# The order of a planned attention-and-gating kernel: one greedy pass against four backward-and-forward passes

## Chip, core and metric

The kernel runs on one core of a Trainium2 chip. The metric is the device time of one execution in microseconds (us). TensorE is called PE here and in the rows, VectorE DVE, ScalarE ACT, GpSimd POOL and SyncE SP. "PEld" is the weight-load side of PE.

## What is computed

The reference chains an attention that keeps only the 32 best scores of each row, a gated block that mixes along the sequence, and a gated block with a causal convolution, all in float32:

```
# q, k, v: 4 x 8 x 576 x 64
scores = scale * np.matmul(q, k.transpose(0, 1, 3, 2))
kth = np.partition(scores, -32, axis=-1)[..., -32:-31]
scores = np.where(scores >= kth, scores, -1e9)
attn = softmax(scores);  x = attn @ v          # laid out as 4 x 576 x 512
h = relu(x @ w_in);  u, v = h[..., :512], h[..., 512:]
v_n = (v - mean(v)) / sqrt(var(v) + 1e-6)
x = (u * (w_spatial @ v_n + b_spatial)) @ w_out
gate = sigmoid(causal_conv5(x, conv_w))
out = (gate * (x @ w_val)) @ w_out2
```

## The kernel before

The attention is cut into 72 units, 18 for each of the 4 batch rows; a unit is two blocks of 128 query rows against all 576 keys. For each unit PE computes the scores in two halves (L453, into the one PSUM tile `sps`), and ACT copies each half to SBUF (L456, `sb`, three buffers). DVE then finds the 32nd largest score of every row: it folds the scores to 168 candidates (L472 to L484, `tm`, `cand`), takes the 8 largest (L494, `t8a`), and three times strikes out the 8 found and takes the next 8 (L505, L507, `t8b`). ACT has meanwhile made the exponentials (L499, `e`, two buffers); DVE masks them with the threshold and sums them (L524), takes the reciprocal of the sum (L529, behind a small ACT copy L528), ACT scales (L532), PE transposes (L541 and L546), ACT copies out (L543, L548), PE multiplies by v (L562), ACT stores into `xt` (L568).

The two gated blocks ("moe" in the code) follow for each batch row as pieces: `xsplit` splits the input into a high and a low part (L623, L625), `piece_v` and `piece_u` are the two halves of the first product (matmuls of helper L603), `piece_sp` the product along the sequence (L706, gated on DVE in L711), `piece_x2`, `conv` (L755), `piece_val` (gated on DVE in L783) and `piece_out`. Their matmuls run as three products of high and low parts. The pieces of one batch row run among the attention units of the next row; those of the fourth row have no attention left beside them. In the first row's attention, the weights, which come as 64-bit numbers, are decoded on ACT, DVE and POOL (`decode`, L292 to L313, and `decode_spatial`) and written to DRAM; `w_load` (L381) loads them again from POOL's queue into one of two buffers `wblk`.

Nothing of the order on the engines is written by hand. Every step is entered with `od.add`: its engine, an estimated duration, the buffers that it reads and writes, a tag with a due time in units (`at`), and in some cases a second engine that could do it (`alt`: the clamp L297 and the low part L298 of `decode`, and for the last batch row the copies and subtractions of the pieces). `Order.plan` plays the steps once through a model of the engines: whenever an engine is free, it takes, of the steps that are ready, the one with the smallest due time plus `AHEAD[tag]`, a table of 45 offsets. `run` then issues the steps in the order in which they were taken. Each engine works its instructions off in that order, so a step that waits holds up all that stand behind it on its engine.

## Time and profile before

| | |
|---|---|
| time, median of 3 runs | 850.48 us (847.73 to 852.22) |
| time of the profiled execution | 852.4 us |
| its span, first to last instruction | 850.5 us |
| busy: PE / DVE / ACT / POOL | 722.2 / 752.4 / 607.0 / 281.0 us |
| mean granted clock of TensorE | 0.927 of full speed |
| instructions | 17268 |

The span is what the trace covers; the time of the same execution holds 1.9 us more around it. Busy times of engines overlap, so they don't add up to the span. An idle time in a row, with what ended it, stands in square brackets.

### The profile page before, as it was taken

To read this page: it belongs to the slowest core of one execution; us is meant where nothing else is said; L and a number is where in the kernel's file an instruction comes from. 1 tells how busy PE (TensorE), PEld (TensorE's weight loads), DVE (VectorE), ACT (ScalarE), POOL (GpSimd) and SP (SyncE) were. 2 spreads that over 40 slices of the span, in tenths; PEclk is the share of its full clock that TensorE was granted. 3 is DMA by queue.
4 is the path that set the end of the run, shared out by engine and by line. 5 is a ranking of instruction groups with operands and counts; after the bars stand their busy time and mean duration, and the time that the engine had idled before them with its cause. 6 is when DMAs were issued, how large, how long until landed. Compare 5 with 4: busy or idle time off the path is not lost.

```text
span 850.5 us, 17268 instructions
## 1 busy us (share of the span) xinstructions
PE 722.2 (85%) x5969; PEld 615.5 (72%) x5969; DVE 752.4 (88%) x2751; ACT 607.0 (71%) x1391; POOL 281.0 (33%) x350
## 2 busy tenths in 40 slices
PE   3153656775979999999999999979999999999987
PEld 2142445554769888987889888857888999878975
DVE  5999999999999999999999999996989999941580
ACT  5477966677887667777986777668786777774341
POOL 5685342576423211222333211213334122322120
PEclk9995766666989999999999999999999999999989
DMA  8777333224114511243224411234035005333501
GB/s 246 255 262 267 100 118 101 77 87 131 51 30 150 188 58 30 99 152 109 79 72 169 156 29 59 91 145 147 16 125 189 25 2 197 139 118 131 207 2 60
DMA packets 46954, 99.25 MB, mean 117 GB/s; under 512 B 22532, under 2 KB 29960, under 8 KB 43272
## 3 DMA queue, kind: packets, MB, share of 16 engines
q0 software_dynamic: 4032, 53.74, 17.7%
q1 hardware_dynamic: 42824, 44.31, 16.6%
q8 instruction: 49, 0.80, 0.4%
q14 instruction: 49, 0.40, 0.2%
HBM read 79.88 MB, written 18.15 MB: 115 GB/s over the span
## 4 chain that ended last, share of the span: by engine, by line
PE 47%; DVE 28%; ACT 15%; POOL 4%; DMA 3%; issue 3%; SPq 0%; POOLq 0%; ACTq 0%; DVEq 0%
PE mp L603 14%; PE xr L562 7%; PE sps L453 6%; PE mp L706 6%; PE mp L755 6%; DVE e L524 5%; DVE tw L505 4%; PE ptp L541 4%; DVE t8b L507 3%; ACT e L532 3%; ACT e L499 2%; ACT pt L543 2%; DVE gate L766 2%; DVE cand L481 2%; DVE tm L473 2%
## 5 line engine op out<-in xcount | busy, mean ns | idle before, releaser
L453 PE MATMUL sps<-k,q 64*128 64x144 f32 (+1 forms) x1280 | 126.7, 341 | 47.9 <-ACT sb L456 40.5
L453 PEld LDWEIGHTS sps<-k,q 64*128 64x128 f32 (+1 forms) x1280 | 90.9, 202 | 78.5 <-ACT sb L456 51.9
L541 PE MATMUL ptp<-ident,e 128*128 128x128 f32 x576 | 94.9, 307 | 51.1 <-ACT e L532 50.4
L524 DVE SCALAR_TENSOR_TENSOR e<-sb,t8b,e 128x576 f32<-128x576 f32 x144 | 128.1, 921 | 1.3 <-ACT e L499 1.3
L541 PEld LDWEIGHTS ptp<-ident,e 128*128 128x128 f32 x576 | 72.5, 155 | 67.2 <-ACT e L532 44.0
L507 DVE MAX8 t8b<-tw 128x8 f32<-128x168 f32 x432 | 120.4, 318 | 0.0
L532 ACT ACTIVATE e<-e,sums 128x576 f32<-128x576 f32 x144 | 106.9, 768 | 15.0 <-DVE sums L529 14.8
L499 ACT ACTIVATE e<-sb,neg 128x576 f32<-128x576 f32 x144 | 106.4, 770 | 0.8
L562 PE MATMUL xr<-pt,vt 128*64 128x128 f32 (+1 forms) x1280 | 91.9, 293 | 17.5 <-ACT pr L548 16.9
L456 ACT ACTIVATE sb<-sps 128x576 f32<-128x576 f32 x144 | 92.7, 644 | 14.2 <-PE sps L453 14.0
L603 PE MATMUL mp<-xh,wblk 128*128 128x288 f32 x448 | 101.5, 305 | 0.0
L562 PEld LDWEIGHTS xr<-pt,vt 128*64 128x64 f32 x1280 | 72.6, 152 | 36.0 <-ACT pr L548 24.1
L505 DVE MATCH_REPLACE8 tw<-t8b,tw 128x168 f32<-128x168 f32 x288 | 88.9, 315 | 0.0
L543 ACT ACTIVATE pt<-ptp 128x512 f32<-128x512 f32 x144 | 80.2, 591 | 2.3 <-PE ptp L541 1.7
L603 PEld LDWEIGHTS mp<-xh,wblk 128*128 128x128 f32 x448 | 74.4, 188 | 5.4 <-issue 0.9
L603 PE MATMUL mp<-wblk,xh 128*128 128x512 f32 (+1 forms) x280 | 75.7, 413 | 0.3 <-ACT xh L623 0.3
L589 POOL TENSOR_TENSOR yl<-ux,yh 128x288 fp32r<-128x288 f32 x31 | 29.2, 944 | 112.4 <-ACT yh L587 108.6
L472 DVE TENSOR_TENSOR tm<-sb 128x576 f32<-128x576 f32 x72 | 57.7, 801 | 9.5 <-ACT sb L456 9.5
L603 PEld LDWEIGHTS mp<-wblk,xh 128*128 128x128 f32 (+1 forms) x280 | 50.6, 190 | 15.1 <-issue 1.4
L603 PE MATMUL mp<-xl,wblk 128*128 128x288 f32 x224 | 61.1, 295 | 0.0
L473 DVE TENSOR_TENSOR tm<-sb 128x576 f32<-128x576 f32 x72 | 58.2, 809 | 0.0
L481 DVE MAX8 cand<-tm 128x8 f32<-128x288 f32 x144 | 57.8, 441 | 0.0
(181 smaller groups left out, 1689.1 us busy)
## 6 DMA issues: line engine op xcount, KB each, us to landing
wblk<-w_out POOLq DMA_DIRECT2D x7, 2048.0 KB, 8.5
wblk<-w_sp POOLq DMA_DIRECT2D x8, 1440.0 KB, 6.6
wblk<-w_inv POOLq DMA_DIRECT2D x4, 2048.0 KB, 8.4
wblk<-w_inu POOLq DMA_DIRECT2D x4, 2048.0 KB, 8.9
wblk<-w_val POOLq DMA_DIRECT2D x4, 2048.0 KB, 8.9
q<-in_qT SPq DMA_DIRECT2D x16, 288.0 KB, 3.9
k<-in_kT SPq DMA_DIRECT2D x16, 288.0 KB, 3.7
stage<-in_w_in SPq DMA_DIRECT2D x8, 512.0 KB, 5.4
```

Of the source, the lines that this page charges most:

```text
L453: nc.tensor.matmul(dst[:, f:f + QUART], lhsT=l, rhs=r[:, f:f + QUART], start=True, stop=True)
L456: od.add("ACT", t_actp(S), lambda c=c: nc.scalar.activation(sb[:, :, CH[c][0]:CH[c][1]], sps[:, :, 0:HALF], AF.Copy), [("sps",)], [("sb", ...
L473: tt(m[:, :, 1, :], sb[:, :, 0:HALF], sb[:, :, HALF:S], op=ALU.min)
L499: od.add("ACT", t_act(S, 1), lambda t=t: nc.scalar.activation(e[:, t, :], sb[:, t, :], AF.Exp, bias=neg[:, t:t + 1], scale=scale), ksb + [ ...
L505: nc.vector.match_replace(w[:, t, :], (t8a if r == 1 else t8b)[:, t, :], (src if r == 1 else w)[:, t, :], LOW)
L507: nc.vector.max(t8b[:, t, :], w[:, t, :])
L524: od.add("DVE", 0.85, lambda t=t, g=g: nc.vector.scalar_tensor_tensor(e[:, t, :], sb[:, t, :], t8b[:, t, 7:8], e[:, t, :], op0=ALU.is_ge, ...
L532: od.add("ACT", t_act(S, 1), lambda t=t, g=g: nc.scalar.activation(e[:, t, :], e[:, t, :], AF.Copy, scale=sums[:, g:g + 1]), [kg[t]], [("e ...
L541: nc.tensor.transpose(pp[:, j, :], e[:, t, REM * t + 128 * j:REM * t + 128 * j + 128], ident)
L543: od.add("ACT", 0.536, lambda: nc.scalar.activation(pt, pp, AF.Copy), [("ptp", g % 2)], [("pt", g % NPT)], ("t", at))
L562: nc.tensor.matmul(xr[64 * o:64 * o + 64, 2, 0:nq], lhsT=vt[:, kt, 64 * o:64 * o + 64], rhs=r, start=kt == 0, stop=kt == KT - 1)
L603: nc.tensor.matmul(ps, lhsT=l, rhs=r, start=m == 0, stop=m == len(ops) - 1)
```

## The change

`plan` becomes two functions. `play` is the old pass with the rule for choosing left open (`key`) and a flag to run it backwards, from the last steps to the first, with predecessors and users exchanged. `plan` first plays with the old key (due time plus `AHEAD`). Then it does four rounds: it plays backwards, taking the steps that ended latest in the preceding forward pass first, and turns the backward start times into latest start times; then it plays forwards with those as priorities. Of the five forward passes it keeps the one that the model says is shortest. A step goes to its second engine only when that engine has nothing of its own ready (in the first pass the clamp L297 has no such penalty). No step is added or removed; the core of the diff:

```
+    ROUNDS = 4
-    def plan(self):
+    def play(self, key, back=False):
...
+        if back:
+            deps, users = users, deps
...
-                    _, _, tag, x = self.ops[i][0][e]
-                    heapq.heappush(rd, (AHEAD.get(tag, 0.0) + x, i))
+                    heapq.heappush(rd, (key(i, e), i))
...
-            if e == "PE":
+            if e == "PE" and not back:
...
+    def plan(self):
+        def first(i, e):
+            return e == next(iter(self.ops[i][0]))
+        def own(i, e):
+            _, _, tag, x = self.ops[i][0][e]
+            return AHEAD.get(tag, 0.0) + x
+        best = run = self.play(own)
+        for _ in range(self.ROUNDS):
+            ends = [t + self.ops[i][0][e][0] for i, (t, e) in enumerate(zip(run[0], run[1]))]
+            late = self.play(lambda i, e: -ends[i] + (0.0 if first(i, e) else 1e4), back=True)
+            by = [late[3] - t - self.ops[i][0][e][0] for i, (t, e) in enumerate(zip(late[0], late[1]))]
+            run = self.play(lambda i, e: by[i] + (0.0 if first(i, e) else self.LATER))
+            best = min(best, run, key=lambda r: r[3])
+        self.start, self.taken, order, self.expected = best
+        return order
```

Lines behind `plan` have numbers 22 higher in the changed kernel (L453 is L475 there). The number of instructions on PE and SP stays; in the decoding, DVE issues 4 fewer (two clamps L297 of 128x256, one of 128x5, one subtraction L298 of 128x512) and POOL those 4 more; in the last batch row one copy goes from ACT and one subtraction from POOL to DVE.

The first place is PE's order where the third batch row's attention hands over to its pieces (560 to 590 us in the profile of before). The rows run from one score half (L453) of a unit to the second half of the unit after it; `mp1` from `wblk0` is `piece_v` of the first block, `mp` from `wblk1` is `piece_out` of the row before. Before:

```order
L453 MATMUL sps_138<-k0_87,q0_83 128x144 x4
...
L541 MATMUL ptp0_139<-ident_78,e0_100 128x128 x4
L541 MATMUL ptp1_140<-ident_78,e0_100 128x128 x4
L546 MATMUL xr_141<-ident_78,e0_100 128x128
L603 MATMUL mp1_143<-wblk0_133,xh_710 128x512 x8
...
L541 MATMUL ptp0_139<-ident_78,e1_101 128x128 x4
L541 MATMUL ptp1_140<-ident_78,e1_101 128x128 x4
L453 MATMUL sps_138<-k0_87,q0_83 128x144 x4
L603 MATMUL mp2_144<-wblk1_134,xh_710 128x512 x8
...
L541 MATMUL ptp0_139<-ident_78,e0_100 128x128 x4
...
L453 MATMUL sps_138<-k0_87,q0_83 128x144 x4
```

And now:

```order
L475 MATMUL sps_138<-k0_87,q0_83 128x144 x4
L625 MATMUL mp1_143<-wblk0_133,xh_740 128x512 x8
...
L475 MATMUL sps_138<-k0_87,q0_83 128x144 x4
L625 MATMUL mp2_144<-wblk1_134,xh_740 128x512 x8
...
L563 MATMUL ptp0_139<-ident_78,e0_100 128x128 x4
L563 MATMUL ptp1_140<-ident_78,e0_100 128x128 x4
L568 MATMUL xr_141<-ident_78,e0_100 128x128
...
L563 MATMUL ptp0_139<-ident_78,e1_101 128x128 x4
L563 MATMUL ptp1_140<-ident_78,e1_101 128x128 x4
L568 MATMUL xr_141<-ident_78,e1_101 128x128
L475 MATMUL sps_138<-k0_87,q0_83 128x144 x4
```

`piece_v` and the next unit's first score half moved ahead of the transposes of `e0`, and one unit's transposes and its products with v moved behind the second score half.

The second place is PE's order at the end of the attention, ahead of the sequence product (L706) of the last batch row; `mp` from `xh` and `wblk0` is `piece_u`, `mp1` and `mp2` from `wblk1` are the last two `piece_v`, and L873 is a small transpose for the final flag. Before:

```order
L603 MATMUL mp0_142<-xh_710,wblk0_133 128x288 x4
L873 MATMUL xr_141<-ident_78,fm_115 1x128
L603 MATMUL mp1_143<-wblk1_134,xh_710 128x512 x8
L603 MATMUL mp1_143<-wblk1_134,xl_711 128x512 x4
L603 MATMUL mp2_144<-wblk1_134,xh_710 128x512 x8
```

And now:

```order
L625 MATMUL mp2_144<-xh_740,wblk0_133 128x288 x4
L625 MATMUL mp1_143<-wblk1_134,xh_740 128x512 x8
L625 MATMUL mp1_143<-wblk1_134,xl_741 128x512 x4
L625 MATMUL mp2_144<-wblk1_134,xh_740 128x512 x8
L625 MATMUL mp2_144<-wblk1_134,xl_741 128x512 x4
```

The two `piece_v` moved ahead of one `piece_u` and of L873; behind them five `piece_u` stand ahead of L706 now, and four did before. From L706 on PE's order is the same.

The third place is DVE's order in the first batch row, from the reciprocal of the sixth unit to the mask of the eighth (both use buffer `e1`). Before, the reciprocal stood four rows behind its mask; between it and the later mask lay 36 rows:

```order
L524 SCALAR_TENSOR_TENSOR e1_101,sums_119<-sb2_99,t8b_110,e1_101 128x576 x2
L513 TENSOR_TENSOR flags_60<-cand_117,t8b_110 128x18
L476 TENSOR_TENSOR cand_117<-tm_114 128x2x144
L477 TENSOR_TENSOR tn4_116<-tm_114 128x288
L529 RECIPROCAL sums_119<-sums_119 128x2
...
L524 SCALAR_TENSOR_TENSOR e1_101,sums_119<-sb1_98,t8b_110,e1_101 128x576 x2
```

Now, from that reciprocal to the same later mask:

```order
L551 RECIPROCAL sums_119<-sums_119 128x2
L527 MATCH_REPLACE tw_118<-t8a1_109,cand_117 128x168 x2
L529 MAX t8b_110<-tw_118 128x8 x2
L494 TENSOR_TENSOR tm_114<-sb2_99 128x2x288
L495 TENSOR_TENSOR tm_114<-sb2_99 128x2x288
...
L498 TENSOR_TENSOR cand_117<-tm_114 128x2x144
L499 TENSOR_TENSOR tn4_116<-tm_114 128x288
...
L324 TENSOR_SCALAR stage10_155<-stage10_155 128x256
L325 SCALAR_TENSOR_TENSOR stage10_155<-stage10_155 128x256
L546 SCALAR_TENSOR_TENSOR e1_101,sums_119<-sb1_98,t8b_110,e1_101 128x576 x2
```

Where "..." stands are two more rounds of L527 and L529. The reciprocal moved from 36 rows ahead of the later mask to 12 rows ahead of it; the same was done to the reciprocals of four more units of this batch row.

## Rows read from the trace of the kernel before

**Rows 1.** The page: busy time, share of the span and instructions of each engine.

```profile
PE 722.2 (85%) x5969; PEld 615.5 (72%) x5969; DVE 752.4 (88%) x2751; ACT 607.0 (71%) x1391; POOL 281.0 (33%) x350
```

**Rows 2.** Stretches: bounds and length, busy time by engine, granted clock, DMA share, GB/s.

```profile
15.00:250.00 235.00, 141.22 (x1060) 111.31 (x1059) 227.78 (x787) 173.84 (x417) 124.73 (x127) 0.77 0.44 139
250.00:560.00 310.00, 303.97 (x2720) 264.40 (x2719) 302.25 (x1184) 238.70 (x538) 78.04 (x106) 0.99 0.31 107
560.00:610.00 50.00, 44.68 (x359) 35.48 (x357) 42.22 (x161) 37.04 (x85) 12.62 (x19) 0.97 0.23 75
610.00:753.00 143.00, 142.24 (x1241) 123.44 (x1240) 137.80 (x536) 108.14 (x245) 44.18 (x54) 1.00 0.31 106
753.00:851.00 98.00, 85.37 (x571) 77.22 (x569) 36.61 (x74) 41.47 (x97) 16.97 (x33) 0.95 0.30 108
```

**Rows 3.** Timeline of PE at the third hand-over (start, duration), and a stretch there.

```profile
568.11 1.78 PE L541 MATMUL ptp<-ident,e 128*128 128x128 f32 x8 [4.67 <-ACT e L532]
569.75 3.08 PE L603 MATMUL mp<-wblk,xh 128*128 128x512 f32 x8
...
584.95 0.76 PE L453 MATMUL sps<-k,q 64*128 64x144 f32 x8
...
568.00:572.00 4.00, 3.89 (x15) 3.22 (x16) 4.00 (x14) 2.80 (x9) 0.00 (x0) 0.57 0.00 0
```

**Rows 4.** Timeline of DVE: the two longest waits for scores behind 15 us.

```profile
586.86 0.76 DVE L472 TENSOR_TENSOR tm<-sb 128x576 f32<-128x576 f32 x1 [5.11 <-ACT sb L456]
...
638.22 0.76 DVE L472 TENSOR_TENSOR tm<-sb 128x576 f32<-128x576 f32 x1 [1.52 <-ACT sb L456]
```

**Rows 5.** Waits: who for whom, us in total, times, longest us.

```profile
DVE sums L529 <- ACT sums L528: 7.0, 10, 1.6
```

**Rows 6.** Groups by form: count, busy us and mean ns, idle before.

```profile
L297 DVE TENSOR_SCALAR stage<-stage 128x256 f32<-128x256 f32 x4 | 1.5, 368 | 0.0
L298 DVE TENSOR_TENSOR stage<-stage 128x512 fp32r<-128x512 f32 x1 | 0.7, 692 | 2.1 <-ACT stage L310 2.1
...
L297 POOL TENSOR_SCALAR stage<-stage 128x256 f32<-128x256 f32 x20 | 23.2, 1161 | 43.1 <-ACT stage L293 42.8
L298 POOL TENSOR_TENSOR stage<-stage 128x512 fp32r<-128x512 f32 x7 | 9.4, 1341 | 2.1 <-ACT stage L310 1.9
```

**Rows 7.** Timeline: one DVE instruction beside a POOL one, and the same alone.

```profile
22.78 1.78 POOL L305 TENSOR_TENSOR stage<-stage 128x512 int32<-128x512 int32 x1
...
23.36 1.82 DVE L473 TENSOR_TENSOR tm<-sb 128x576 f32<-128x576 f32 x1
...
571.11 0.75 DVE L473 TENSOR_TENSOR tm<-sb 128x576 f32<-128x576 f32 x1
```

**Rows 8.** Timeline: the load ahead of the last sequence product, and its start on PE.

```profile
775.05 0.63 POOL L381 DMA_DIRECT2D wblk<-w_sp  x1 [0.26 <-issue]
...
781.81 0.54 PE L706 MATMUL sps<-wblk,yh 128*128 128x288 f32 x2 [1.00 <-DMA wblk<-w_sp]
```

**Rows 9.** Timeline of DVE: one strike-out round, and one unit's folding.

```profile
566.74 0.07 DVE L505 MATCH_VALUE_LOAD tw<-t8b,tw 128x8 f32 x1
...
567.81 0.07 DVE L505 MATCH_VALUE_LOAD tw<-t8b,tw 128x8 f32 x1
...
570.45 0.74 DVE L472 TENSOR_TENSOR tm<-sb 128x576 f32<-128x576 f32 x1
...
572.58 0.81 DVE L481 MAX8 cand<-tm 128x8 f32<-128x288 f32 x2
```

**Rows 10.** Timeline: from reciprocal to exponentials in the first batch row; an ACT wait.

```profile
112.69 0.14 DVE L529 RECIPROCAL sums<-sums 128x2 f32<-128x2 f32 x1
...
115.45 0.42 PE L546 MATMUL xr<-ident,e 128*128 128x128 f32 x1
...
114.31 1.43 ACT L499 ACTIVATE e<-sb,neg 128x576 f32<-128x576 f32 x2
...
30.11 0.63 ACT L310 ACTIVATE stage<-stage 128x512 fp32r<-128x512 f32 x1 [4.19 <-POOL stage L305]
```

More of the change, by code (lines that the diff above doesn't have):

```diff
@@ L74, in add @@
         return i
-    def plan(self):
+    def play(self, key, back=False):
         n = len(self.ops)
-        left = [len(o[1]) for o in self.ops]
+        deps = [list(o[1]) for o in self.ops]
         users = [[] for _ in range(n)]
-        for i, o in enumerate(self.ops):
-            for d in o[1]:
-                users[d].append(i)
+        for i, d in enumerate(deps):
+            for j in d:
+                users[j].append(i)
+        if back:
+            deps, users = users, deps
+        left = [len(d) for d in deps]
         ready_at = [0.0] * n
@@ L89, in plan @@
                 ready.setdefault(e, [])
-        taken = [None] * n
-        start = [0.0] * n
+        taken, start, order = [None] * n, [0.0] * n, []
         def release(i):
@@ L98, in plan @@
                 release(i)
-        order = []
         w = w_busy = 0
@@ L122, in plan @@
                 if not taken[i]:
-                    _, _, tag, x = self.ops[i][0][e]
-                    heapq.heappush(rd, (AHEAD.get(tag, 0.0) + x, i))
+                    heapq.heappush(rd, (key(i, e), i))
             _, i = heapq.heappop(rd)
-            ways, deps, lat = self.ops[i]
             taken[i] = e
@@ L129, in plan @@
             order.append(i)
+            ways, _, lat = self.ops[i]
             dur = ways[e][0]
-            if e == "PE":
+            if e == "PE" and not back:
                 while (w + 1) * self.WINDOW <= t:
@@ L139, in plan @@
             free[e] = t + dur
-            end = t + dur + lat
             for u in users[i]:
                 left[u] -= 1
-                ready_at[u] = max(ready_at[u], end + (self.SAME if e in self.ops[u][0] else self.SYNC).get(e, 0.0))
+                a, b = (i, u) if not back else (u, i)
+                eng = e if not back else next(iter(self.ops[u][0]))
+                sync = (self.SAME if eng in self.ops[b][0] else self.SYNC).get(eng, 0.0)
+                ready_at[u] = max(ready_at[u], t + dur + self.ops[a][2] + sync)
                 if not left[u]:
                     release(u)
-        self.taken, self.start = taken, start
-        self.expected = max(free.values())
+        return start, taken, order, max(free.values())
+    def plan(self):
[12 more added lines that the diff above has]
+        self.start, self.taken, order, self.expected = best
         return order
```

## The prediction

> **What bounds the kernel now.** I read the page first, then the busy times by stretch, then the timeline of the engine that is fullest and of the one that it waits for. On the page the reader is to see two nearly full engines: DVE is busy for 88% of the span and PE for 85% [rows 1]; the rest has time to spare. An average hides stages with other limits, so the stretches come next [rows 2]. From 15 to 753 us, where the last unit's masking ends on DVE, DVE is busy for 227.78 + 302.25 + 42.22 + 137.80 = 710.0 of 738 us; it is idle for 28 us in all. From 753 us on DVE has 36.6 us of work in 98 us, and PE 85.4: there the chain of matmuls and small copies of the last batch row sets the end. So the time is DVE's work ahead of 753 us, plus the waits in it, plus a tail on PE. A new order can only change three things: the 28 us of waits, the few instructions that change engines, and the waits in the tail. PE looks just as full between 250 and 753 us (303.97 of 310 us, 142.24 of 143), but a busy time of PE holds matmuls that queue behind each other's operands; DVE's waits tell whether PE is late, and there are few of them. In the first 235 us PE is busy for 141 us only and DVE for 227.8 of 235: DVE sets the pace there.
>
> **The waits on DVE, and what the new order does to each.** The longest is at the third hand-over: DVE waits 5.11 us for a unit's scores [rows 4]. The cause is on PE [rows 3]: it stood idle for 4.67 us, until 568.11, because the transposes of `e0` at the head of its queue waited for ACT's scaling (L532), and then ran `piece_v` and other work ahead of the second score half, which started at 584.95. The granted clock of 568 to 572 us is 0.57: behind that idle time PE ran most of these 4 us at its lower level, 1.2 GHz, and eight transposes took 1.78 us. In the new order `piece_v` stands ahead of those transposes, where the 4.67 us were idle, and one unit's transposes and products fall behind the second score half. The score half is then early by at least the 4.67 us, plus what was moved behind it, so DVE's 5.11 us should go: I take -5.1, with 0 as the other end if the scores come as late for another reason. The weights and inputs of that `piece_v` are not what held it: it ran straight behind the transposes. Late next would be the mask, which waits for ACT's exponentials; it stood right ahead of this wait and costs what it costs now.
>
> The wait of 1.52 us at 638.22 [rows 4] is of the same kind, and the new order puts one unit's products with v behind two score halves there: -1.0, between 0 and -1.5.
>
> The reciprocal L529 waits for a chain that begins with the mask just ahead of it, and DVE stands still for 7.0 us in 10 such waits [rows 5]. How much work DVE has between mask and reciprocal can be counted in the order, instruction by instruction: 17 of the 72 units have under 0.9 us there before, 9 have now. By that share 7.0 x 8 / 17 = 3.3 us would go; since a wait also depends on what ACT is doing, I take -2.0, between 0 and -3.3.
>
> **The instructions that change engines.** In the decoding DVE loses two clamps of 128x256, one of 128x5 and one subtraction: 2 x 0.37 + 0.69 = 1.4 us by their means [rows 6], and some 0.2 for the small one. POOL gets 2 x 1.16 + 1.34 = 3.7 us; it is busy for 125 of 235 us there, so it has room. But POOL's work isn't free for DVE: L473 took 1.82 us beside a POOL instruction of 1.78 us, and 0.75 alone [rows 7], so 1.07 us were lost on one overlap. If each of the four moved instructions meets such a DVE instruction, 4.3 us come back. The term lies between -1.6 and +2.7; most of POOL's instructions in this stretch overlap DVE work that is not slowed, so I stay near the lower end, at -0.8.
>
> The Trainium skill (page "SBUF - State Buffer", section "Who interferes with whom") says that a DVE instruction with two SBUF inputs and a POOL instruction that reads SBUF exclude each other for the whole instruction, and that the one issued second is fully blocked. The row of 1.82 us agrees as to direction; by the rule alone, with all 3.7 us of the moved POOL work in DVE's way, this term would be 3.7 - 1.6 = +2.1 instead of -0.8, and the time 2.9 us more than I forecast.
>
> **The tail.** PE waits 1.00 us for the weights of the sequence product (L706 at 781.81); that load was issued at 775.05, once the last `piece_v` had released its buffer [rows 8]. With one `piece_u` moved behind it, the load starts earlier by that piece, and PE has the piece to run while it waits: -1.0, between 0 and -1.6. Behind L706 PE's order is the same, so nothing else changes there. The copy and the subtraction that DVE takes over in this batch row lie in a stretch where DVE is idle for 61 of 98 us, beside PE work; if that cover were gone they would cost under 1 us.
>
> **What the new order adds.** Five reciprocals of the first batch row now stand close ahead of the mask two units later. That mask needs the exponentials of its unit, these need buffer `e1` (or `e0`) free, and that needs the scaling and the transposes behind the late reciprocal. From the reciprocal to the mask DVE now has three strike-out rounds of 1.07 us and a folding of 2.13 [rows 9], 5.3 us, and two decode instructions: about 5.9 us for the unit that I show; for the other four I count 6.5, 6.5, 7.2 and 8.9 in the same way. The chain: from the reciprocal at 112.69 to the end of the last transpose at 115.87 are 3.2 us, and two exponentials are 1.43 [rows 10], 4.6 us with nothing in between and some 5 with the handing over. On ACT's queue decode steps stand between, and such a step waited 4.19 us for POOL once [rows 10]. Queued behind the mask on DVE is everything. The cost has 0 as its lower end; at the upper end each of the five chains takes 5 + 4.2 = 9.2 us, over by 3.3 + 2.7 + 2.7 + 2.0 + 0.3 = 11.0 us. I take +2.5, near the lower end, because most ACT waits of this kind are shorter than that one and the order leaves all five above 5.
>
> **The sum.** -5.1 - 1.0 - 2.0 - 0.8 - 1.0 + 2.5 = -7.4 us, from the time of the profiled execution: 852.4 - 7.4 = 845.0. That execution is 1.9 us above the median of the runs (850.48), so against the median I expect 850.5 - 7.4 = 843.1, say 843.
>
> **Rivals.**
> The gains are absorbed: with DVE's waits gone at one place, PE, which is busy for 98% and more of two of these stretches, is late at the next, and DVE waits there. For it speaks how full PE is behind 250 us; against it, that DVE's waits in 250 to 560 us are 7.8 us only, although PE is as full there. Then the 6.1 us at the two hand-over places come back, and the sum is -1.3: 849.
> The late reciprocals cost more: the order is fitted to the model's durations, with nothing in reserve. The place is the first batch row, the price is above. The five chains have 5.9 + 6.5 + 6.5 + 7.2 + 8.9 = 35.0 us of cover, and the gains are 9.9 us without the +2.5; so from (35.0 + 9.9) / 5 = 9.0 us per chain on, the change loses. With a chain of 10 to 11 us (5, the 4.19 us wait, and ACT work in between) it loses 5 to 10 us: 856 to 861, say 857.
> More is gained than I can see place by place: the new order is drawn for all 28 us of DVE waits. If half of the 14 us that my terms don't name go as well, and nothing new comes: 850.5 - 9.9 - 7 = 834.
> That the change does nothing is excluded: the pass kept could have been the first, but the orders differ from the first attention unit on.
>
> **How the numbers follow.** Chances: the likeliest case 0.50 (840 to 847), absorbed 0.24 (847 to 853), slower 0.14 (854 to 861), more gained 0.12 (830 to 840). Half a per cent is 4.25 us, about what a measurement of this kernel can tell from no change: faster means below 846.2, slower above 854.7. Faster: 0.12 and 0.46 of the first case, 0.58; same: 0.24 and 0.04, 0.28; slower 0.14. The range leaves out about one in ten on either side: from 834 to 855.
>
> **What would show it.** In the profile of the changed kernel: at the third hand-over no PE wait of over 1 us for L532 ahead of L563, a granted clock near 1, and no DVE wait of over 2 us ahead of L494; reciprocal waits (L551 behind L550) of 3 to 5 us in all; no PE wait ahead of L728; and in the first 235 us DVE waits ahead of L546, for ACT's L521, of 1 to 5 us in all, where there were none. It is wrong if these waits exceed 10 us, if POOL's longer list stretches DVE's busy time in the first 235 us by more than 3 us, or if DVE's idle time between 250 and 753 us is not below 16 us (20.7 now).

## The result, and the profile after

The changed kernel takes 844.05 us (median of 6 runs, 839.99 to 844.29) against 850.56 us (6 runs, 847.73 to 852.34): a ratio of 0.9912, with a 95% interval of 0.9886 to 0.9938, so 6.5 us less by the medians. The forecast was 843. The profiled execution after is the fastest of its six (839.99 us, span 838.1), the profiled one of before is 1.9 us above its median; the two traces lie 12.4 us apart, of which about 6 are the choice of executions. Small differences between the two traces are therefore read with care below, and a size is taken from runs where there are any. In kernel.py every line behind the planner stands 22 further down than before: L494 is what L472 was.

The line of busy times on the page of the changed kernel, which answers to [rows 1]:

```profile
PE 708.3 (85%) x5969; PEld 605.2 (72%) x5969; DVE 754.7 (90%) x2749; ACT 602.8 (72%) x1390; POOL 290.6 (35%) x353
```

The busy times by stretch of the changed kernel, up to the last unit's masking (741 us) and behind it, as in [rows 2]:

```profile
15.00:250.00 235.00, 139.60 (x1101) 109.48 (x1102) 227.05 (x806) 174.41 (x421) 129.84 (x133) 0.75 0.45 145
250.00:560.00 310.00, 302.65 (x2737) 262.49 (x2735) 308.38 (x1187) 238.10 (x542) 87.05 (x106) 1.00 0.31 105
560.00:610.00 50.00, 45.13 (x350) 36.84 (x349) 44.04 (x168) 39.39 (x90) 15.20 (x25) 0.93 0.22 70
610.00:741.00 131.00, 130.21 (x1179) 114.68 (x1177) 128.99 (x499) 98.91 (x221) 33.34 (x43) 1.00 0.34 117
741.00:838.00 97.00, 86.55 (x587) 78.56 (x586) 38.85 (x81) 43.05 (x102) 19.01 (x36) 0.96 0.29 103
```

DVE is idle for 7.95, 1.62, 5.96 and 2.01 us in the four stretches ahead of the tail. In [rows 2] it was 7.22, 7.75, 7.78 and 5.20. The largest drop, 6.1 us, lies between 250 and 560 us, a stretch for which the forecast had named no term but a share of the reciprocals'.

Little of that drop is time gained. The next two rows run from the end of unit 20's mask to that of unit 54's (units counted from 0), before and after; the first figure behind the bounds is the length, and the third busy time is DVE's:

```profile
258.69:581.19 322.50, 311.70 (x2773) 269.74 (x2772) 314.05 (x1232) 247.47 (x557) 78.52 (x109) 0.99 0.29 101
...
253.65:574.38 320.73, 309.46 (x2778) 266.81 (x2776) 319.11 (x1231) 245.09 (x555) 88.39 (x108) 1.00 0.32 108
```

DVE's idle time fell there from 8.45 to 1.62 us, and the time only from 322.5 to 320.7: DVE issues 1231 instructions where it issued 1232, and they take 5.1 us more. It takes 321.9 to 322.6 us in the traces of three kernels that have the order of before there, and 320.7 to 322.2 in four that have the new one (the others are those of the experiments below). Instructions of the same form are longer on average, as the mask and the third step of the folding show, before and after:

```profile
L524 DVE SCALAR_TENSOR_TENSOR e<-sb,t8b,e 128x576 f32<-128x576 f32 x69 | 58.9, 883 | 1.3 <-ACT e L499 1.3
L476 DVE TENSOR_TENSOR cand<-tm 128x288 f32<-128x288 f32 x33 | 15.6, 471 | 0.0
...
L546 DVE SCALAR_TENSOR_TENSOR e<-sb,t8b,e 128x576 f32<-128x576 f32 x68 | 60.9, 917 | 0.0
...
L498 DVE TENSOR_TENSOR cand<-tm 128x288 f32<-128x288 f32 x33 | 18.4, 556 | 0.0
```

POOL is busy for 88.4 us in that stretch where it was 78.5, and single rows show DVE's instructions longer beside POOL's [rows 7]; that POOL lengthens all of these is likely, but no run here isolates it.

The waits of DVE in the changed kernel (who for whom, us in total, times, longest):

```profile
DVE sums L551 <- ACT sums L550: 5.5, 7, 1.8
DVE tm L494 <- ACT sb L478: 5.4, 3, 2.4
DVE stage L324 <- POOL stage L319: 4.0, 4, 1.2
...
DVE ux L733 <- PE mp L728: 1.5, 4, 0.4
...
DVE gate L805 <- PE mp L625: 0.6, 3, 0.3
```

The reciprocals' waits went from 7.0 to 5.5 us [rows 5]. There are three waits for scores, and none is 5 us long [rows 4]. Between 250 and 752 us DVE had also waited 5.1 us in 11 short waits ahead of the gating and the sequence product (L805 and L733 now), all but one of 0.4 us by the profile for PE's products; there, 0.2 us are left (the two rows above count the tail too).

At the third hand-over the wait was not removed, it was split. The timeline of DVE in the changed kernel shows its two parts:

```profile
577.18 0.76 DVE L494 TENSOR_TENSOR tm<-sb 128x576 f32<-128x576 f32 x1 [2.35 <-ACT sb L478]
...
587.54 0.76 DVE L494 TENSOR_TENSOR tm<-sb 128x576 f32<-128x576 f32 x1 [1.52 <-ACT sb L478]
```

On ACT's timeline, this stands ahead of the copy for which the first of them waits:

```profile
574.42 0.20 ACT L550 ACTIVATE sums<-sums 128x2 f32<-128x2 f32 x1 [2.28 <-DVE e L546]
574.53 0.58 ACT L565 ACTIVATE pt<-ptp 128x512 f32<-128x512 f32 x1
575.01 0.27 ACT L570 ACTIVATE pr<-xr 128x128 f32<-128x128 f32 x1
575.17 1.44 ACT L554 ACTIVATE e<-e,sums 128x576 f32<-128x576 f32 x2
576.50 0.65 ACT L478 ACTIVATE sb<-sps 128x576 f32<-128x576 f32 x1
```

PE's timeline in the same microseconds, with its idle time in brackets:

```profile
571.05 0.33 PE L568 MATMUL xr<-ident,e 128*128 128x128 f32 x1 [1.99 <-ACT xt L590]
571.31 1.15 PE L475 MATMUL sps<-k,q 64*128 64x144 f32 x8
575.33 1.12 PE L584 MATMUL xr<-pt,vt 128*64 128x64 f32 x16 [2.88 <-ACT pr L570]
```

Two stretches of 4 us there, with the granted clock as the third figure from the end:

```profile
568.00:572.00 4.00, 2.01 (x18) 1.65 (x17) 4.00 (x23) 3.56 (x8) 0.25 (x1) 0.94 0.92 303
572.00:576.00 4.00, 1.12 (x16) 0.78 (x16) 2.55 (x5) 1.72 (x6) 1.03 (x1) 0.50 0.63 256
```

PE no longer waits for the scaling there [rows 3], but it stands idle for 1.99 and 2.88 us, nearly as long as before (4.67), for other copies of ACT; the granted clock of 572 to 576 us is 0.50, the lower level (1.2 GHz), behind the idle time. The scores on which DVE waits were through PE by 572.5. Their copy, L478, ran at 576.50, because ACT takes its instructions in order: ahead of it stood the sum step L550, which waited 2.28 us for DVE's own mask, then two copies and two scalings. So DVE waited for a copy that was queued behind a wait for DVE. About 1 of the 2.28 us is that mask's own length, beside a subtraction on POOL:

```profile
571.75 1.28 POOL L647 TENSOR_TENSOR xl<-xt,xh 128x512 fp32r<-128x512 f32 x1 [4.03 <-ACT xh L645]
...
571.78 1.86 DVE L546 SCALAR_TENSOR_TENSOR e<-sb,t8b,e 128x576 f32<-128x576 f32 x1
...
573.57 0.81 DVE L546 SCALAR_TENSOR_TENSOR e<-sb,t8b,e 128x576 f32<-128x576 f32 x1
```

In the tail PE waits for no weights any more [rows 8]; the product that did so starts at 770.85 straight behind the matmul ahead of it, and the tail takes 96.8 us where it took 98.4.

### The profile page after: what moved, and what is told of

Same layout as the page of the kernel before. It is cut to its first block, busy times and chain, and to the rows that moved or that the text cites. A ratio compares the mean times of both kernels' runs of the same rounds, so it can differ in the third digit from the quotient of the medians.

```text
span 838.1 us, 17270 instructions
## 1 busy us (share of the span) xinstructions
PE 708.3 (85%) x5969; PEld 605.2 (72%) x5969; DVE 754.7 (90%) x2749; ACT 602.8 (72%) x1390; POOL 290.6 (35%) x353
## 4 chain that ended last, share of the span: by engine, by line
DVE 51%; PE 23%; ACT 6%; issue 2%; POOL 1%; DMA 0%; POOLq 0%; DVEq 0%; ACTq 0%
DVE tw L527 10%; DVE e L546 10%; PE mp L625 8%; DVE t8b L529 7%; PE mp L728 4%; DVE tm L494 4%; DVE cand L503 4%; DVE tm L495 3%; DVE cand L506 3%; PE xr L584 3%; DVE t8a L516 2%; DVE cand L498 2%; PE sps L475 2%; DVE tn L499 2%; DVE gate L788 2%
## 5 line engine op out<-in xcount | busy, mean ns | idle before, releaser
L475 PE MATMUL sps<-k,q 64*128 64x144 f32 (+1 forms) x1280 | 126.4, 341 | 85.2 <-ACT sb L478 77.9
L475 PEld LDWEIGHTS sps<-k,q 64*128 64x128 f32 (+1 forms) x1280 | 90.4, 201 | 116.0 <-ACT sb L478 88.6
L546 DVE SCALAR_TENSOR_TENSOR e<-sb,t8b,e 128x576 f32<-128x576 f32 x144 | 132.5, 945 | 0.1
L529 DVE MAX8 t8b<-tw 128x8 f32<-128x168 f32 x432 | 120.3, 318 | 0.0
L478 ACT ACTIVATE sb<-sps 128x576 f32<-128x576 f32 x144 | 93.0, 646 | 19.6 <-PE sps L475 17.2
L584 PE MATMUL xr<-pt,vt 128*64 128x128 f32 (+1 forms) x1280 | 87.8, 281 | 18.0 <-ACT pr L570 17.7
L584 PEld LDWEIGHTS xr<-pt,vt 128*64 128x64 f32 x1280 | 68.3, 144 | 36.4 <-ACT pr L570 23.6
L527 DVE MATCH_REPLACE8 tw<-t8b,tw 128x168 f32<-128x168 f32 x288 | 88.8, 314 | 0.0
L625 PE MATMUL mp<-wblk,xh 128*128 128x512 f32 (+1 forms) x280 | 73.9, 406 | 1.1 <-POOL stage L327 1.1
L494 DVE TENSOR_TENSOR tm<-sb 128x576 f32<-128x576 f32 x72 | 58.8, 817 | 5.6 <-ACT sb L478 5.4
L625 PE MATMUL mp<-xl,wblk 128*128 128x288 f32 x224 | 60.9, 294 | 0.0
L495 DVE TENSOR_TENSOR tm<-sb 128x576 f32<-128x576 f32 x72 | 60.4, 838 | 0.0
```

The costliest lines, as they stand in the source:

```text
L475: nc.tensor.matmul(dst[:, f:f + QUART], lhsT=l, rhs=r[:, f:f + QUART], start=True, stop=True)
L478: od.add("ACT", t_actp(S), lambda c=c: nc.scalar.activation(sb[:, :, CH[c][0]:CH[c][1]], sps[:, :, 0:HALF], AF.Copy), [("sps",)], [("sb", ...
L494: tt(m[:, :, 0, :], sb[:, :, 0:HALF], sb[:, :, HALF:S], op=ALU.max)
L527: nc.vector.match_replace(w[:, t, :], (t8a if r == 1 else t8b)[:, t, :], (src if r == 1 else w)[:, t, :], LOW)
L529: nc.vector.max(t8b[:, t, :], w[:, t, :])
L546: od.add("DVE", 0.85, lambda t=t, g=g: nc.vector.scalar_tensor_tensor(e[:, t, :], sb[:, t, :], t8b[:, t, 7:8], e[:, t, :], op0=ALU.is_ge, ...
```

## Experiments: the change in parts

Three kernels take a part of the new order. Both orders are drawn; all steps that the one starts ahead of a time stand in it, all others behind them in the order and on the engines of the other. In the first the new order (`best`) leads up to 250 us; in the other two `p, q` is `old, best` and the time 400 and 700 us.

```diff
-        best = run = self.play(own)
+        old = best = run = self.play(own)
...
-        self.start, self.taken, order, self.expected = best
-        return order
+        p, q = best, old
+        ahead = {i for i, t in enumerate(p[0]) if t < 250.0}
+        self.taken = [(p if i in ahead else q)[1][i] for i in range(len(self.ops))]
+        return [i for i in p[2] if i in ahead] + [i for i in q[2] if i not in ahead]
```

> All steps that the new plan starts before 250 us stand in the new order, all others behind them in the order of before (the join falls at units 21 and 22 of the 72). Theory 1, the gains add up place by place: the lead that the trace of the changed kernel has at unit 21 (5.0 us between the two profiled executions) stays to the end, so 845.5 us; scaled to the difference of the medians (6.5 of the 12.4 us between those two executions) 848. Theory 2, an early gain is taken back: the engines behind the join are as full as before, DVE waits there for PE, and the time is 850.5 or more.

> The converse: the order of before for all steps that the old plan starts before 400 us (unit 37), the new order behind them. Theory 1: the lead from unit 37 to the last mask grew by 3.9 us and the tail gave 1.5, so 5.4 us: 845; scaled as above 847.6. Theory 2, the whole gain is made by DVE's waits for scores and products from 400 us on, and the first half gives nothing that lasts: 844, as the changed kernel.

> Only the steps that the old plan starts at 700 us or later stand in the new order: the last three units and the tail of the last batch row. By the trace the tail gave 1.5 us (98.35 to 96.8 behind the last mask): 849. Theory 3, the planner's own figures are right: it puts this order at 842.1 against 848.9 for the order of before, so 843.7.

| part in the new order | median, us | ratio to before, 95% interval | us by the ratio |
|---|---|---|---|
| up to 250 us | 848.22 | 0.9974 (0.9959 to 0.9989) | -2.2 |
| from 400 us on | 847.17 | 0.9951 (0.9932 to 0.9969) | -4.2 |
| from 700 us on | 848.96 | 0.9979 (0.9966 to 0.9992) | -1.8 |
| all | 844.05 | 0.9912 (0.9886 to 0.9938) | -7.5 |

The parts add up within their intervals: -2.2 and -4.2 make -6.4; the whole is -7.5 by its ratio, with 2.2 to either side, and -6.5 by the medians. No kernel takes the steps between 250 and 400 us alone; -1.1 is left for them, less than the interval. So theory 1 holds, and a gain made early is not taken back (theory 2). Of the second part's 4.2 us the last three units and the tail are 1.8, so the attention units from 400 us on, third hand-over included, gave about 2.4. The traces say nearly the same of the hand-over alone: from the end of unit 54's mask to that of unit 59's DVE took 54.2 us before and 51.4 after; to that of unit 60's it took 67.3 and 63.4. In the trace of the second part's kernel the same stretches took 52.8 and 64.7, so one trace gives these gains to within some 1.4 us. Ahead of it nothing was gained: from the end of unit 37's mask to that of unit 54's DVE took 160.7 us before (161.8 in the first part's kernel, with the same order there) and 162.2 after, though its idle time there fell from 4.2 us to none. The planner's own figure for the tail (-6.8) was not met.

Where the first part's gain lies is not settled. The stretch of the first 15 us of the kernel with the new order up to 250 us:

```profile
0.00:15.00 15.00, 4.24 (x26) 3.22 (x28) 7.45 (x12) 8.88 (x17) 6.14 (x13) 1.00 0.76 257
```

The same stretch of the kernel with the order of before up to 700 us:

```profile
0.00:15.00 15.00, 4.92 (x32) 3.91 (x32) 5.99 (x12) 8.07 (x13) 4.78 (x12) 1.00 0.84 262
```

In the first of these DVE is busy for 1.46 us more, and for 0.7 more between 15 and 250 us (227.34 against 226.61): 2.2 us less idle time in all, as many as the runs gained. But in the first 15 us it issues 12 instructions in both, and the added busy time is length, not work. Two rows of the first kernel, one form of clamp (L321 there):

```profile
9.02 0.43 DVE L321 TENSOR_SCALAR stage<-stage 128x512 f32<-128x512 f32 x1 [1.54 <-ACT stage L317]
...
10.64 1.42 DVE L321 TENSOR_SCALAR stage<-stage 128x512 f32<-128x512 f32 x1
```

Up to the end of unit 20's mask DVE is idle for 15.2 us in the first kernel and 17.5 in the second, and for 15.6 after and 17.1 before; the mask ends at 255.4, 255.9, 253.7 and 258.7 us. That goes the way of the 2.2 us, but single traces differ by as much in this stage (see the last section).

The fourth kernel takes the order after one round (`ROUNDS = 1`).

> One round backwards and forwards in place of four; the order kept is another one. The planner's own figures: 848.9 for the order of before, 835.6 for this one, 833.5 for the one of four rounds. Theory 3, the planner's figures rank orders rightly: 844.05 + 2.1 = 846, scaled by 6.5 / 15.4 = 845. Rival, differences of this size are chance on the chip: anywhere from 838 to 852, and not tied to the figure.

It took 850.73 us, ratio 1.0001 (0.9986 to 1.0016): nothing is left of the 13 us that the planner's figure had promised. In its trace the reciprocals wait most (10.9 us in 15 waits, against 5.5 in 7 in the changed kernel). The planner's figure doesn't rank these orders; theory 3 fell.

## Experiments: the hand-over, POOL, and late reciprocals

Two kernels move single steps of the new order. `find` gives the steps of a kind and unit, `move` puts them behind another step in the order; a unit is counted from 0 here. The first has the first `move` only.

```diff
...
+        def move(steps, behind):
...
+            for i in steps:
+                order.remove(i)
+            order[order.index(behind) + 1:order.index(behind) + 1] = steps
+        move(find("rACT", 54) + find("rDVE", 54) + find("mACT", 54), find("sACT", 55)[1])
+        move([find("VPE", 49)[0]], find("sPE", 56)[1])
+        move(find("rACT", 57), find("mDVE", 57)[1])
+        move(find("rDVE", 57), find("fDVE", 58)[3])
+        move([find("sPE", 60)[1]], find("mDVE", 59)[1])
+        move([find("sACT", 60)[1]], find("rACT", 59)[0])
```

> The new order with one place changed. At the third hand-over of the changed kernel DVE waits 2.35 us for scores (577.18); the copy of these scores on ACT stands behind the sum step of unit 54, which itself waits 2.28 us for DVE's mask (574.42), and behind two copies and two scalings. Here the sum step, the reciprocal and the scalings of that unit stand behind the score copy. Theory 4, the wait is that step's place in ACT's queue, and what is taken away there lasts: 844.05 - 2.35 = 841.7. Theory 5, the next score wait (1.52 us at 587.54) grows by as much, as PE's order sets the pace there: 843.2 to 844.05.

> As the one before, and three more places: a second score half ahead of the piece_v that stood before it (DVE wait of 1.52 us at 587.54), a sum step and its reciprocal moved apart (1.81 us at 610.27), and a second score half and its copy earlier (1.55 us at 627.89). Theory 4: 844.05 - 2.35 - 1.52 - 1.81 - 1.55 = 836.8. Theory 5, engines that full give back elsewhere what is taken away by hand: between 842 and 846. The planner's own model has this order 5.7 us above the one that it kept: by theory 3 (the planner's figures are right) 847 to 850.

The first took 840.22 us, ratio 0.9884 (0.9866 to 0.9903), by the ratios 2.4 us less than the changed kernel, where 2.35 were expected. The intervals of the two ratios overlap, so the runs alone don't show it; the traces do. The wait at 577 us is gone, a mask waits 0.34 us more for exponentials, and the waits behind it are as long as they were. From the end of unit 54's mask to that of unit 55's DVE takes 9.37 us, and 11.63 in the changed kernel (11.8 and 13.0 in the kernels with the clamps on DVE and with the new order from 400 us on, which have the new order here); from there to the last mask it takes 155.29 and 155.30. So this wait was the sum step's place in ACT's queue, and the 2.26 us taken away there lasted. The second took 841.1 us (0.9894, 0.9877 to 0.9912): the other three places gave nothing. In its trace of DVE the wait at 587 us, which a score half moved ahead of `piece_v` on PE was to remove, has grown from 1.52 to 2.65 us, and a mask waits 1.42 for exponentials:

```profile
583.17 0.82 DVE L562 SCALAR_TENSOR_TENSOR e<-sb,t8b,e 128x576 f32<-128x576 f32 x1 [1.42 <-ACT e L537]
587.38 0.76 DVE L510 TENSOR_TENSOR tm<-sb 128x576 f32<-128x576 f32 x1 [2.65 <-ACT sb L494]
```

At that place DVE waits 1.13 + 1.42 = 2.55 us more. Not all of this is shown to come from the move: the mask of the same unit waits 1.54 us in the kernel with the new order from 400 us on, where no step was moved. The waits at 610 and 628 us are gone (3.36 us), and new ones stand behind them (0.89, 0.28, 0.37, and 0.55 where 0.19 was), so the other two places won about 1.5. From the end of unit 54's mask to the last one DVE takes 166.2 us, and 164.7 in the kernel with one place moved: the three together gave nothing. In these two kernels the wait that was a step's place in a queue could be moved away for nothing; where PE was late, moving steps only moved the wait.

The third kernel puts the clamps of the decoding on DVE.

```diff
+        for i, o in enumerate(self.ops):
+            if list(o[0]) == ["DVE", "POOL"] and o[0]["DVE"][2] == "DDVE":
+                self.taken[i] = "DVE"
```

> The new order, but all clamps of the decoding on DVE; the change itself had moved three from DVE to POOL, here 29 go the other way. DVE gains 22 x 0.37 + 4 x 0.43 + 3 x 0.18 = 10.4 us of work, POOL loses about 36 us (29 clamps, mean 1.25). Theory 6, POOL's work stretches DVE's by a small share of its length: between 15 and 250 us five DVE groups of two inputs are stretched by 18.7 us beside 129.8 us of POOL, 0.14 us for one of POOL; 36 us less give 5.2 back, the sum is +5.2: 849.3. Rival, each POOL clamp holds DVE up for its whole length: 844.05 + 10.4 - 36 = 818. Second rival, POOL's clamps cost DVE nothing: 854.5.

It took 842.5 us, ratio 0.9909 (0.9892 to 0.9927), the same as the changed kernel. Its stretch of 15 to 250 us:

```profile
15.00:250.00 235.00, 139.41 (x1085) 109.36 (x1084) 228.83 (x827) 173.58 (x417) 90.63 (x102) 0.80 0.44 142
```

POOL has 39 us less to do there than in the changed kernel; DVE has the 29 clamps, about 9 us (the 128x256 ones took 0.305 us on average), and its busy time grew by 1.8 us (by 5.9 over the whole kernel, from 754.7 to 760.6), its idle time fell by as much, from 7.95 to 6.17. So the added work is paid back, by less stretching and by shorter waits. That POOL's clamps hold DVE up for their whole length (818 us) is excluded, and that they cost it nothing (854.5) as well. Theory 6 is 6.8 us too high: it had priced the stretch by the mean of all of POOL's work, and left out the waits; how much is owed to each is not settled.

The fourth makes the reciprocals later than either order (`COVER` is 3.0 us); `late` holds a reciprocal and all steps that depend on it, and those of them up to the new place go there with it.

```diff
+        for u in range(1, 16):
+            r, m = find("rDVE", u)[0], find("mDVE", u + 2)[0]
+            k, cover = order.index(m), 0.0
+            while cover < self.COVER:
+                k -= 1
+                if self.taken[order[k]] == "DVE" and order[k] != r:
+                    cover += self.ops[order[k]][0]["DVE"][0]
...
+            a = order.index(r)
+            held = [i for i in order[a:k] if i in late]
+            order[a:k] = [i for i in order[a:k] if i not in late] + held
```

> The new order, but 15 reciprocals of the first batch row (units 1 to 15) stand so late that DVE has only 3.0 us of planned work from there to the mask two units later. Theory 7, the chain of reciprocal, scaling, transposes and exponentials takes about 5 us, as the prediction put it: each mask waits some 2 us, 15 x 2 = 30 us: 874. Rival, the chain is hidden at this distance too, since the exponentials don't stand behind it: 844 to 846. Second rival, the chain is longer, 7 us as in the planner's model, and 15 x 4 = 60 us are lost: 905.

It took 904.27 us (1.0646, 1.0623 to 1.0669), 60 us more than the changed kernel: the number of the second rival, but not its account, as the waits show. The two longest groups of DVE's waits in it:

```profile
DVE stage L351 <- POOL stage L346: 36.9, 12, 6.9
DVE e L573 <- ACT e L548: 23.4, 10, 5.6
```

One reciprocal and the mask two units later on DVE:

```profile
118.13 0.15 DVE L578 RECIPROCAL sums<-sums 128x2 f32<-128x2 f32 x1
...
125.42 0.82 DVE L573 SCALAR_TENSOR_TENSOR e<-sb,t8b,e 128x576 f32<-128x576 f32 x1 [4.14 <-ACT e L548]
```

ACT between the two:

```profile
118.31 1.44 ACT L581 ACTIVATE e<-e,sums 128x576 f32<-128x576 f32 x2 [1.48 <-DVE sums L578]
...
124.44 0.28 ACT L617 ACTIVATE xt<-xr 128x128 f32<-128x128 f32 x1 [2.48 <-PE xr L611]
124.62 1.43 ACT L548 ACTIVATE e<-sb,neg 128x576 f32<-128x576 f32 x2
```

From reciprocal to mask are 7.3 us, not 5: on ACT the exponentials stand behind a copy that waits 2.48 us for PE. Over the nine of the 15 masks that wait, it is 4.0 to 10.5 us. And the masks' waits are the smaller part. The larger, 36.9 us, is DVE waiting for POOL's clamps; these wait for ACT's decode steps, which are queued behind the scalings that wait for the late reciprocal, as on POOL's timeline here:

```profile
136.54 1.06 POOL L346 TENSOR_SCALAR stage<-stage 128x256 f32<-128x256 f32 x1 [5.04 <-ACT stage L342]
```

In the changed kernel the closest of the late reciprocals stands 6.07 us ahead of its mask on DVE:

```profile
111.22 0.15 DVE L551 RECIPROCAL sums<-sums 128x2 f32<-128x2 f32 x1
...
117.29 0.81 DVE L546 SCALAR_TENSOR_TENSOR e<-sb,t8b,e 128x576 f32<-128x576 f32 x1
```

Neither this mask nor those of the other four wait there. On ACT the second of the exponentials that this mask needs ends at 116.18 us, 5.0 us behind the reciprocal:

```profile
115.41 0.77 ACT L521 ACTIVATE e<-sb,neg 128x576 f32<-128x576 f32 x1
```

So the danger was real, and the order kept clear of it.

## Experiments: what the planner's figure counts

The planner's figures had failed for the tail, for one round, and for the four places. The suspect was its rule for PE's clock, a factor of 1.95 on matmuls behind a stretch with little work on PE. Three kernels draw the order without it; the second and third also add small random numbers to the priorities and take the last round's order (the second's lines are shown; the third has another seed, 1.0 and 0.2 us, and six rounds).

```diff
-                dur *= 1.95 if cold else 1.0
+                dur *= 1.0
```

```diff
-        best = run = self.play(own)
+        rng = random.Random(31)
+        a, b = ([rng.gauss(0, s) for _ in self.ops] for s in (0.3, 0.05))
+        run = self.play(lambda i, e: own(i, e) + a[i])
...
-            run = self.play(lambda i, e: by[i] + (0.0 if first(i, e) else self.LATER))
-            best = min(best, run, key=lambda r: r[3])
+            run = self.play(lambda i, e: by[i] + b[i] + (0.0 if first(i, e) else self.LATER))
-        self.start, self.taken, order, self.expected = best
+        self.start, self.taken, order, self.expected = run
```

> The planner without its rule that a matmul takes 1.95 times as long after a stretch with little work on PE; everything else, the four rounds too, as in the changed kernel. Played without the rule, the planner's figures are 839.5 for the order of before, 832.4 for the changed kernel and 827.2 for this order; with the rule 848.9, 833.5 and 879.9. Theory 8, the rule misleads the planner, since a matmul that runs slowly where PE has time to spare costs nothing: 844.05 - 5.2 = 839. Theory 3, the planner's figure with the rule counts: this order is 46 us slower, 890. Rival, differences between good orders are chance: 840 to 851.

> As the one before, with small random numbers added to the priorities (0.3 us forwards at the start, 0.05 us in the rounds); this seed is the best of some hundred by a play with durations varied by 8 per cent and DVE held up for half of each overlap with POOL. Without the clock rule the planner's figure is 820.5, 11.9 below the changed kernel. Theory 8: 844.05 - 11.9 = 832, with half of it in the tail. Rival, the best of many by a model is the best of its errors: 838 to 845.

> A second order of the same kind from another seed, with larger numbers (1.0 and 0.2 us) and six rounds: figure 821.2 without the clock rule, 873.9 with it (the one before: 849.3 with it). Theory 8: 833, like the one before. Theory 3, the rule counts: some 25 us slower than the one before. Rival, chance: 838 to 851.

They took 844.23 us (0.9925, 0.9904 to 0.9945), 832.52 us (0.9802, 0.9778 to 0.9826) and 841.78 us (0.9903, 0.9881 to 0.9924). By the figure with the rule they should have been 46, 16 and 40 us slower than the changed kernel; one is equal, one 11.5 us faster (9.4 by the ratios), one about equal. So the rule's surcharge isn't there in the time. But the figure without it doesn't rank them either: it saw 5.2 us that didn't come in the first, was near for the second (11.9), and saw 11.2 in the third, where 2.3 came by the medians and 0.8 by the ratios. Of theory 8 only the one half stands, that the surcharge isn't paid; the other, that the figure without it can be trusted, fell with the first and the third. What the trace shows is where the second one is faster. Its stretches from 250 us on, and its tail from the last mask (739.8 us) on:

```profile
250.00:560.00 310.00, 308.17 (x2772) 267.59 (x2772) 305.27 (x1185) 240.77 (x544) 85.53 (x108) 1.00 0.33 112
560.00:610.00 50.00, 50.00 (x438) 42.31 (x437) 49.78 (x198) 45.75 (x111) 22.53 (x31) 1.00 0.28 93
610.00:735.00 125.00, 124.62 (x1109) 108.50 (x1108) 124.67 (x481) 92.40 (x209) 33.62 (x40) 1.00 0.34 119
...
739.80:829.00 89.20, 80.19 (x555) 73.44 (x554) 39.39 (x83) 37.73 (x89) 17.11 (x33) 0.97 0.27 96
```

The changed kernel's tail, cut at its last mask in the same way:

```profile
741.30:838.00 96.70, 86.25 (x585) 78.25 (x583) 38.55 (x81) 43.05 (x102) 19.01 (x36) 0.96 0.29 102
```

PE is never idle between 560 and 610 us, where it was idle for 4.87 us in the changed kernel; between 250 and 560 us it is idle for 1.83 us instead of 7.35. The last mask ends only 1.5 us earlier than in the changed kernel's trace, but the tail is 7.5 us shorter, with 30 matmuls and 6.1 us of PE's work less in it. So PE had done work of the last batch row earlier. Between 250 us and the tail its idle time fell from 13.0 to 2.2 us.

The last kernel moves the sum steps of units 18 and 19 of this order right behind their masks.

```diff
...
+        for u in (18, 19):
...
+            r = find("rACT", u)[0]
+            order.remove(r)
+            order.insert(max(map(order.index, find("mDVE", u))) + 1, r)
```

> The first perturbed order with two steps moved. DVE's longest waits there between 15 and 740 us apart from one at 40 us are for the sums of units 18 and 19 (counted from 0): 1.37 us at 242.14 and 2.68 at 253.10; the sum step on ACT stands behind a scaling that waits 1.32 us for POOL, and behind four steps and a wait of 0.92 us for PE. Here each stands right behind the two masks of its unit. Theory 4, a wait that is a step's place in ACT's queue goes when the step is moved, and what is saved lasts: 832.5 - 1.4 - 2.7 = 828.4. Theory 5, PE is busy for 308 of the 310 us that follow, so DVE waits there instead: 831 to 833.

It took 832.7 us, 0.9779 (0.9759 to 0.9799), against 0.9802 of the order that it changes; the intervals overlap, so between theories 4 and 5 the runs don't decide. In its trace the two waits of together 4.05 us are down to 0.54, and 2.5 us are won from unit 17 to unit 20; then a new wait on DVE takes 1.4 of them back:

```profile
270.80 0.17 DVE L561 RECIPROCAL sums<-sums 128x2 f32<-128x2 f32 x1 [1.43 <-ACT sums L560]
```

Either of the two last orders beats both kernels, by 2.0 and 2.2% against before.

## Why the prediction came out right

The forecast was 843, the time 844.05, and its direction and range held. The sum was -7.4 and 6.5 us came, but the terms were off in both directions, and cancelled: that the number came so near is luck in good part.

**The hand-over, -5.1 and -1.0: mis-sized, with a wrong next step.** PE did take `piece_v` where it had been idle, and DVE's 5.11 us went. The step that failed is "Late next would be the mask, which waits for ACT's exponentials". Late next was the score copy, behind the sum step on ACT's queue (2.35 us; the kernel that moves this step shows it), and then PE's second score half (1.52). The wait at 638 us stayed (1.55 us at 627.89). From 400 us on the units gave 2.4 us in the runs, and the hand-over 2.8 (to unit 59) to 4.0 (to unit 60) in the traces, not 6.1. So some of it came back, as the rival of the absorbed gains had it, but not for its reason: DVE's first new wait was for ACT's queue and not for PE, and in the units ahead of the hand-over DVE did not wait at all, its instructions took longer. Four of the signs given were wrong: the clock was 0.50 in one stretch, one wait ahead of L494 is over 2 us, the reciprocals' waits are above 5 us, and no mask waits for exponentials in the first 235 us, where 1 to 5 us were foreseen. The sign of DVE's idle time between 250 and 753 us below 16 us was met (9.6 up to the last mask), but most of that fall was no gain, as the rows from unit 20 to unit 54 show.

**Reciprocals, -2.0:** 7.0 us of waits became 5.5 in the traces; -1.5, if all of it is time gained.

**Changed engines, -0.8:** nothing that can be measured. Moving 29 clamps the other way, ten times as many, leaves the time where it is, so neither -1.6 nor +2.7 is likely to have come of four instructions. The Trainium skill (page "SBUF - State Buffer", section "Who interferes with whom") would let an instruction of POOL block one of DVE's for its whole length where they compete; single rows agree [rows 7], but taken over all 29 clamps, with each in DVE's way, it would give an estimated 818 us, where 842.5 were measured.

**The tail, -1.0:** -1.8 (0.7 to 2.9) by its own kernel, which has the last three units in it as well, and PE's wait for the weights is gone, as said.

**Late reciprocals, +2.5:** nothing. The count of DVE's work from reciprocal to mask was right (5.9 us counted for the closest, 6.07 in the trace). The chain of 5 us was right for ACT's queue as it stands there (5.0 in the trace); with another queue it is 7.3 in the one shown and 10.5 at most, and what is lost then is lost mostly by decode steps. So the rival's chain of 10 to 11 us occurs once in that kernel, and not in the order that was forecast.

**Not in the sum:** the gain of the first part, -2.2 by its own kernel, where the late reciprocals and the changed engines made +1.7 together; what it comes from stays open. And the waits for PE's products between 250 and 752 us, 5.1 us in 11 short ones, of which 0.2 are left. The prediction had them among the 14 us of waits that no term named, and gave a gain from there a chance of 0.12. The waits did go, but the time hardly followed: from unit 20's mask to unit 54's DVE lost 6.8 us of idle time and the kernel 1.8 us. The prediction had taken DVE's work ahead of the tail as fixed but for the moved instructions, so that each microsecond of waits would be one of time; it was not, since DVE's instructions became longer.

## What to carry to other kernels

Where an order is redrawn, don't take idle time that is gone for time gained: here most of eleven short waits went, 4.9 us in all, and the stretch in which most of them lay became less than 2 us shorter, because the engine's instructions took longer. Compare the time between the same two steps in both traces, beside the waits. When a long wait is to go, read the queue of the engine that delivers, in order, down to the step that waits for the waiting engine itself; here that one decided what was late next, and moving it was cheap. And where two engines are nearly full and one of them has a tail, count the second one's idle time ahead of the tail too: the fastest order here has a tail 7.5 us shorter, and 10.8 us less of PE's idle time between 250 us and the tail.

## What the runs showed that was not expected

The decode stage doesn't take the same time twice. The kernel that keeps the order of before up to 700 us had the same instructions in the same order there as before, and ended unit 17's mask 2.5 us earlier in its profiled execution (231.4 against 233.9 us); the last two kernels, equal up to there, lie 2.0 us apart. Differences of 2 us between two traces at one place of this stage mean nothing on their own, and what was gained there had to be told by medians. Behind it the traces agree better: from unit 37's mask to unit 53's it is 149.9 us in all three kernels that have the order of before there.

What the planner's rule adds for PE's lower clock level did not come: by the figure with the rule the first order drawn without it should have been 46 us slower than the changed kernel, and the two are equal (844.23 and 844.05 us). What that level costs in the decode stage they don't show. Between 15 and 250 us the granted clock, a mix of both levels, was 0.75 in the changed kernel and 0.83 in the other, yet in the other unit 20's mask ends 12.5 us later (266.2 against 253.7 us), with DVE idle for 25.3 us up to there instead of 15.6. It catches up behind 560 us: from unit 53's mask to unit 59's it takes 53.3 us, the changed kernel 60.9.
